# Cosine attention followed by a low-rank mixer: another order for the normalisation of the first heads, and six products spread over the MLP tiles

## The chip, the cores and the metric

One core of one Trainium2 chip. The metric is the time of one execution on the device in microseconds (us), the median of several runs. In three profiles (e2, e9 and c2) the matmul clock was granted at half for 3.4 us inside the ramp, from about 22 to 27 us; where it bears on a reading the text says so. A profiled execution's span is some 2 us below the timed figure of the same run (603.2 against 604.94 for the kernel before), so spans are compared with spans and times with times.

The profile's names: PE is TensorE (matmuls), ACT is ScalarE, DVE is VectorE, POOL is GpSimd, SP is SyncE. L577 is a line of the kernel; `attn<-sc` is the tile written and the tile read. A load *lands* when its data has arrived. The *ramp* is the time until PE is full, and the *rows* are the normalised rows of q and k.

## The reference, cut to what matters

```python
# q, k, v: 8 x 12 x 448 x 64 (batch, heads, tokens, width); C = 768
q_n = q / (norm(q) + 1e-6);  k_n = k / (norm(k) + 1e-6)
attn = softmax(q_n @ k_n.T / tau)          # tau = 0.1
x    = (attn @ v), heads side by side      # 8 x 448 x 768
u    = x + (x.T @ U @ V).T                 # low rank, 32, along the tokens
out  = u + relu(u @ w_ch1) @ w_ch2         # 768 -> 3072 -> 768
```

## The kernel before

The kernel doesn't fix the order of its instructions by hand. It hands operations with durations, dependencies and priorities to a small planner that simulates the engines and emits one order for each. A change of a dependency or priority re-plans the rest of the program, and once planned, each engine runs its own list in order.

Batch 0's twelve heads are normalised in four groups: the first pair (heads 0 and 1), the second pair, a third group of four heads and a fourth of four. Each group is squares, sums, ln and exp (for the root), an addition, a reciprocal, products with the rows:

```python
def squares(b, g, ld, ops, lo, ii, ss, pr, on, hold):
    for i in ii:                                   # q, k
        for a0 in range(0, g, G // 2):
            sq = Slot(r_sq, 1)                     # a ring of two buffers
            o = Op(on, ..., deps=[ops[i], *hold], acq=[sq], prio=pr + 0.2, fast=True)
            ...                                    # Square on ACT or x*x on DVE
            red.append(plan.add(Op("DVE", ..., reduce_sum(...),
                deps=[o], acq=[ss], rel=[sq], prio=pr + 0.1)))

def stats_first(ld, ops):                          # the first pair
    for i in range(2):
        done[i], up = scales(0, 0, 2, ld, ops, 0, (i,), inv, -1 - 0.1 * i, ("DVE", "ACT")[i])

# [...] order of the front:
second = load_qk(0, 2, 4, uses=2)
ld, ops, _ = load_qk(0, 4, 8)
begun = stats_first(*first[:2])
stats(0, 2, 4, *second, hold=begun)
xn_set.append(fill(memset of the third xn buffer, prio=0.2, deps=begun))
zf = fill(memset of the landing area of U and V, prio=0.1, acq=[uv], deps=begun)
stats(0, 4, 8, ld, ops, 0, hold=got[0, 0, "qkT"][2])
load_v0()
ld, ops, _ = load_qk(0, 8, 12)
late = stats(0, 8, 12, ld, ops, 0)
```

After batch 0's attention the MLP's long products start ("the block" below) and PE is full from there on. At MLP tile 9 the low-rank term is added for all tokens at once, three token tiles by two halves:

```python
def by_tokens(us, A, X):
    for i in range(3):
        for c0, c1 in ((0, CH), (CH, C)):
            mm = Slot(r_mm, 1)                     # a ring of three PSUM banks
            o = plan.add(Op("PE", ..., V_sb[...] x A[:, c0:c1] -> mm))
            plan.add(Op("DVE", ..., u = mm + X, deps=[o], rel=[mm, X], prio=2))
...
    if b == 0 and f == 9:
        by_tokens(us, *state["first"])
```

## Time and profile before

| | before |
|---|---|
| time, median of 3 runs | 605.15 us (604.89 to 605.44) |
| PE busy | 586.4 of 603.2 us |
| last exp of batch 0 ends (ACT) | 37.85 us |
| first long product of the MLP block (PE) | 41.3 us |

How to read it: in timelines each line has its start, its length (of a run of equal instructions), engine, source line, operation, tile, shapes, count, and in brackets the idle time before it with what ended it. The lines are in the prediction.

### The profile page before, as it was taken

What the parts mean: (1) busy time and instruction counts of PE and PEld (TensorE: products, weight loads), DVE (VectorE), ACT (ScalarE), POOL (GpSimd) and SP (SyncE); (2) the same over time, 40 slices, a digit from 0 to 9 for tenths busy, and PEclk for the clock granted to TensorE, in tenths of its full rate; (3) what the DMA queues carried; (4) which work ended last, traced back from release to release, by engine and by line L of the source; (5) the groups of instructions that cost most, each with busy time, mean ns of one, the idle gap of its engine ahead of it and who ended that gap; (6) DMA issues with size and microseconds to landing.
All of it is one profiled execution on the core that took longest, in us unless ns stands there. A gap on an engine that the chain in (4) does not pass through costs nothing.

```text
span 603.2 us, 11528 instructions
## 1 busy us (share of the span) xinstructions
PE 586.4 (97%) x4725; PEld 347.0 (58%) x4725; DVE 300.6 (50%) x728; ACT 276.9 (46%) x598; POOL 115.2 (19%) x175
## 2 busy tenths in 40 slices
PE   3899999999999999999999999999999999999997
PEld 1565666555565665666445666566545666654565
DVE  8979749989999988554731244014300210110011
ACT  5877652488874277316741067505642025014300
POOL 8246334062706116000600000000000000000000
PEclk9999999999999999999999999999999999999999
DMA  9999999999999959725922133030002110310021
GB/s 144 193 188 112 204 201 107 150 173 136 159 152 155 149 102 154 95 57 90 123 29 66 52 74 47 1 93 27 15 1 53 52 40 1 90 42 1 0 53 54
DMA packets 150165, 54.81 MB, mean 91 GB/s; under 512 B 115040, under 2 KB 150112, under 8 KB 150112
## 3 DMA queue, kind: packets, MB, share of 16 engines
q0 software_dynamic: 72864, 25.73, 38.4%
q1 hardware_dynamic: 77184, 28.32, 24.4%
q8 instruction: 37, 0.61, 0.4%
q14 instruction: 16, 0.13, 0.1%
q10 hardware_dynamic: 64, 0.02, 0.0%
HBM read 52.25 MB, written 11.01 MB: 105 GB/s over the span
## 4 chain that ended last, share of the span: by engine, by line
PE 93%; DVE 2%; ACT 2%; POOL 1%; DMA 1%; issue 0%; ACTq 0%; POOLq 0%
PE mm L794 36%; PE mm L760 35%; PE sc L572 10%; PE av L592 8%; PE mm L684 1%; PE tp L374 1%; DMA v_nat<-in_v_dram 1%; DVE xn L536 1%; PE mm L649 1%; POOL v_nat L429 1%; ACT attn L577 1%; PE sc L760 0%; POOL qk_nat L396 0%; DVE ss L461 0%; ACT qkT L824 0%
## 5 line engine op out<-in xcount | busy, mean ns | idle before, releaser
L760 PE MATMUL mm<-uT,w_sb 128*128 128x512 bf16 (+1 forms) x1134 | 241.3, 353 | 0.2 <-DVE u_nat L734 0.2
L794 PE MATMUL mm<-w_sb,relu 128*128 128x384 bf16 (+1 forms) x1368 | 231.3, 323 | 0.0
L577 ACT ACTIVATE attn<-sc 128x448 bf16<-128x448 f32 x336 | 164.6, 552 | 110.9 <-PE av L592 58.2
L794 PEld LDWEIGHTS <-relu 128*128 128x128 bf16 x1368 | 132.7, 98 | 86.1 <-issue 0.2
L760 PEld LDWEIGHTS <-w_sb 128*128 128x128 bf16 x1152 | 111.8, 98 | 102.7 <-issue 1.8
L783 ACT ACTIVATE relu<-mm 128x512 bf16<-128x512 f32 (+1 forms) x158 | 86.8, 549 | 129.3 <-PE mm L760 128.7
L803 DVE TENSOR_TENSOR O_sb<-mm,u_nat 128x384 f32<-128x384 f32 (+1 forms) x57 | 31.2, 549 | 210.8 <-PE mm L794 207.4
L572 PE MATMUL sc<-qkT 128*128 128x448 bf16 x336 | 102.7, 356 | 3.7 <-ACT attn L577 2.0
L592 PEld LDWEIGHTS <-attn 128*128 128x128 bf16 x1536 | 62.1, 98 | 17.8 <-issue 2.5
L418 POOL DMA_DIRECT2D v_nat<-in_v_dram x98 | 63.2, 655 | 31.7 <-DMA w_sb<-in_moe_w_ch_dram 15.8
L592 PE MATMUL av<-v_nat,attn 128*128 128x65 bf16 x1536 | 66.6, 194 | 0.8 <-DMA v_nat<-in_v_dram 0.4
L461 DVE TENSOR_REDUCE ss<-sq 112x8 f32<-112x512 bf16 x96 | 63.1, 673 | 0.2
L536 DVE TENSOR_TENSOR xn<-qk_nat,inv 112x512 bf16<-112x512 bf16 x94 | 60.9, 681 | 2.4 <-DMA qkT<-xn 2.2
L396 POOL DMA_DIRECT2D qk_nat<-in_q_dram x24 | 17.2, 718 | 136.5 <-DVE xn L536 117.0
L572 PEld LDWEIGHTS <-qkT 128*128 128x128 bf16 x336 | 28.9, 98 | 22.1 <-issue 7.3
L601 DVE TENSOR_TENSOR X_sb<-av,rd 128x256 bf16<-128x256 f32 x96 | 40.1, 419 | 1.6
L599 DVE RECIPROCAL rd<-av 128x4 f32<-128x4 f32 x96 | 17.1, 179 | 37.6 <-PE av L592 36.9
L457 DVE TENSOR_TENSOR sq<-qk_nat 112x512 bf16<-112x512 bf16 x87 | 33.7, 415 | 0.0
L698 DVE TENSOR_TENSOR u_nat<-mm,X_sb 128x384 bf16<-128x384 f32 x36 | 19.2, 553 | 15.4 <-PE mm L684 15.1
L785 DVE TENSOR_SCALAR relu<-mm 128x384 bf16<-128x384 f32 (+1 forms) x31 | 18.7, 604 | 12.8 <-PE mm L760 12.0
L374 PE MATMUL tp<-ident,xn 112*128 112x112 bf16 x144 | 11.9, 226 | 7.8 <-DVE xn L536 7.6
L474 ACT ACTIVATE ln<-ss 112x32 f32<-112x32 f32 (+2 forms) x26 | 6.0, 231 | 27.3 <-DVE ss L461 27.1
(61 smaller groups left out, 172.5 us busy)
## 6 DMA issues: line engine op xcount, KB each, us to landing
qk_nat<-in_q_dram POOLq DMA_DIRECT2D x23, 224.0 KB, 5.2
qk_nat<-in_k_dram POOLq DMA_DIRECT2D x23, 224.0 KB, 6.3
w_sb<-in_moe_w_ch_dram POOLq DMA_DIRECT2D x4, 1152.0 KB, 14.6
w_sb<-in_moe_w_ch_dram POOLq DMA_DIRECT2D x8, 576.0 KB, 15.8
out_dram<-O_sb SPq DMA_DIRECT2D x15, 168.0 KB, 2.2
out_dram<-O_sb SPq DMA_DIRECT2D x16, 144.0 KB, 2.1
out_dram<-O_sb SPq DMA_DIRECT2D x16, 120.0 KB, 2.0
out_dram<-O_sb SPq DMA_DIRECT2D x16, 96.0 KB, 2.2
```

Source lines behind the costliest of these rows:

```text
L418: nc.gpsimd.dma_start(out=vb[p0:p0 + s1 - s0, hs, j, 0:D], in_=v[b, hs].rearrange("h (s c) d -> c s h d", c=SC)[c, s0:s1]),
L457: nc.vector.tensor_mul(y, x, x)
L461: lambda i=i, a0=a0, a1=a1, sq=sq: nc.vector.reduce_sum(ss.tile[:, i, a0:a1, :].rearrange("p h c -> p (h c)"), sq.tile[:, 0:a1 - a0, :].re ...
L536: nc.vector.tensor_mul(dst, src, sc)
L572: nc.tensor.matmul(out=sc.tile[:, 0:S], lhsT=kT[:, 128 * m:128 * (m + 1)], rhs=qkT.tile[:, 8:12, :].rearrange("p c s -> p (c s)"), start=T ...
L577: exps[m] = plan.add(Op("ACT", act_t(S), lambda sc=sc, m=m: nc.scalar.activation(out=attn.tile[:, m, off:off + S], in_=sc.tile[:, 0:S], fu ...
L592: nc.tensor.matmul(out=av.tile[:, t, 0:D + 1], lhsT=attn.tile[:, m, 128 * t:128 * (t + 1)], rhs=v_t[b % 2][:, h, j, 0:D + 1], start=(j == ...
L601: muls.append(plan.add(Op("DVE", dve_t(256), lambda av=av, rd=rd, h=h: nc.vector.tensor_mul(X.tile[:, :, h * D:(h + 1) * D], av.tile[:, :, ...
L760: o = plan.add(Op("PE", pe_t(n), lambda cc=cc: nc.tensor.matmul(out=mm.tile[:, 0:n], lhsT=w1_sb[:, cc, f * 128:(f + 1) * 128], rhs=uT.tile ...
L783: nc.scalar.activation(out=relu.tile[:, f, 0:n], in_=mm.tile[:, 0:n], func=AF.Relu)
L794: nc.tensor.matmul(out=mm.tile[:, 0:c1 - c0], lhsT=relu.tile[:, f, i * 128:(i + 1) * 128], rhs=w2_t[:, f, c0:c1], start=(f == 0), stop=(f ...
L803: nc.vector.tensor_add(out=O.tile[:, 0:w], in0=mm.tile[:, 0:w], in1=us[i].tile[:, c0:c1]),
```

## The change

The intent: ACT squares both halves of the first pair; the second pair's sums and rows come next on DVE, ahead of two memsets and of the third group (`then`, `hold`), so that ACT gets its second pair of heads sooner; products with v are planned after v has landed; and the six products of `by_tokens` stand one at every second MLP tile.

```diff
-    done[i], up = scales(..., ("DVE", "ACT")[i])
+    done[i], up = scales(..., "ACT")
-    deps=[o], acq=[ss], rel=[sq], prio=pr + 0.1)))                # the sums
+    deps=[o, *then], acq=[ss], rel=[sq], prio=pr + 0.1)))
-    stats(0, 2, 4, *second, hold=begun)
-    xn_set.append(fill(..., prio=0.2, deps=begun))
-    zf = fill(..., prio=0.1, acq=[uv], deps=begun)
-    z  = fill(lambda: nc.vector.memset(V_sb, 0.0), 500, prio=-1.3)
+    begun_2 = stats(0, 2, 4, *second, hold=begun[:2], then=begun)
+    xn_set.append(fill(..., prio=0.41, deps=begun))
+    z  = fill(lambda: nc.vector.memset(V_sb, 0.0), 500, prio=3, deps=begun)
+    zf = fill(..., prio=0.5, acq=[uv], deps=begun)
-    stats(0, 4, 8, ld, ops, 0, hold=got[0, 0, "qkT"][2])
+    stats(0, 4, 8, *third, hold=last_exp["first"], then=begun_2)
-    LATE = 8.0                                # v: planned as landed after 2.0
+    LATE, VLATE = 8.0, 3.2                    # v: after 3.2; batch 0's q, k: 2.5 for 2.0
-    plan.add(Op("PE", 0.033, fn, ...          # a product with v, as planned
+    plan.add(Op("PE", 0.09 if b == 0 and p == 0 else 0.033, fn, ...
-    if b == 0 and f == 9:
-        by_tokens(us, *state["first"])
+    if b == 0 and 9 <= f < 21 and f % 2:
+        by_tokens(us, *state["first"], (f - 9) // 2)
[... the planner's rule for squares on ACT, the order of calls, signatures]
```

More of the change, by code (lines that the diff above doesn't have):

```diff
@@ L155, in run @@
                                 continue
-                            if e == "ACT" and o.fast and free["DVE"] <= t + 1e-9:
+                            if e == "ACT" and o.fast and "/" in o.eng and free["DVE"] <= t + 1e-9:
                                 continue
@@ L398, in load_qk @@
             in_=src[b, h0:h1].rearrange("h (s c) d -> s h (c d)", c=SC)),
-            (h1 - h0) * (0.31 if b else 0.35) + (1.2 if b == 0 and h0 == 4 and i == 0 else 0.0), acq=[ld], late=2.0 if b == 0 else LATE) for i, src in enumerate((q, k))]
+            (h1 - h0) * (0.31 if b else 0.35) + (1.2 if b == 0 and h0 == 4 and i == 0 else 0.0), acq=[ld], late=2.5 if b == 0 else LATE) for i, src in enumerate((q, k))]
         return ld, ops, lo
@@ L431, in part @@
                 in_=v[0, hs].rearrange("h (s c) d -> c s h d", c=SC)[c, s0:s0 + n]),
-                n * (0.0055 if hs.step == 2 else 0.011)))
+                n * (0.0055 if hs.step == 2 else 0.011), late=VLATE))
         for j in range(3):
@@ L440, in load_v0, with squares @@
             got[0, h, "v"] = ops
-    def squares(b, g, ld, ops, lo, ii, ss, pr, on, hold):
+    def squares(b, g, ld, ops, lo, ii, ss, pr, on, hold, then):
         red = []
@@ L464, in squares, with scales @@
                         axis=AX.X),
-                    deps=[o], acq=[ss], rel=[sq], prio=pr + 0.1)))
+                    deps=[o, *then], acq=[ss], rel=[sq], prio=pr + 0.1)))
         return red
-    def scales(b, h0, h1, ld, ops, lo, ii, inv, pr, on, hold=()):
+    def scales(b, h0, h1, ld, ops, lo, ii, inv, pr, on, hold=(), then=()):
         g = h1 - h0
         ss, ln, nv = Slot(r_ss, 1), Slot(r_ln, 1), Slot(r_ln, 1)
-        red = squares(b, g, ld, ops, lo, ii, ss, pr, on, hold)
+        red = squares(b, g, ld, ops, lo, ii, ss, pr, on, hold, then)
         w = slice(ii[0], ii[-1] + 1)
@@ L484, in scales, with stats @@
         return o, up
-    def stats(b, h0, h1, ld, ops, lo, hold=()):
+    def stats(b, h0, h1, ld, ops, lo, hold=(), then=()):
         pr = 0.3 + 0.03 * h0 if b == 0 else 4
         inv = Slot(r_inv, h1 - h0)
-        o, _ = scales(b, h0, h1, ld, ops, lo, (0, 1), inv, pr, "DVE" if b else "ACT/DVE", hold)
+        o, _ = scales(b, h0, h1, ld, ops, lo, (0, 1), inv, pr, "DVE" if b else "ACT/DVE", hold, then)
         for p in range(h0 // 2, h1 // 2):
@@ L499, in stats_first @@
         for i in range(2):
-            done[i], up = scales(0, 0, 2, ld, ops, 0, (i,), inv, -1 - 0.1 * i, ("DVE", "ACT")[i])
+            done[i], up = scales(0, 0, 2, ld, ops, 0, (i,), inv, -1 - 0.1 * i, "ACT")
             ups.append(up)
@@ L580, in attention @@
         last_exp[b] = exps[5]
+        if b == 0 and p == 0:
+            last_exp["first"] = [exps[1]]
         muls = []
@@ L595, in fn @@
                             rhs=v_t[b % 2][:, h, j, 0:D + 1], start=(j == 0), stop=(j == 3))
-                    o = plan.add(Op("PE", 0.033, fn,
+                    o = plan.add(Op("PE", 0.09 if b == 0 and p == 0 else 0.033, fn,
                         deps=need + got[b, h, "v"] + attn_set + [v_set[b % 2]] if first else (), acq=[av] if first else [],
@@ L723, in stage0, with by_tokens @@
         return us, uT, ut
-    def by_tokens(us, A, X):
-        for i in range(3):
-            for c0, c1 in ((0, CH), (CH, C)):
+    def by_tokens(us, A, X, part):
+        for i in range(part // 2, part // 2 + 1):
+            for c0, c1 in [((0, CH), (CH, C))[part % 2]]:
                 mm = Slot(r_mm, 1)
@@ L878, in att @@
     def att(b):
-        X = Slot(r_X, 0)
-        muls = []
-        for p in range(NPAIR):
+        X = Slot(r_X, 0) if b else X0
+        muls = [] if b else list(muls0)
+        for p in range(0 if b else 1, NPAIR):
             muls += attention(b, p, X)
@@ L889 @@
     second = load_qk(0, 2, 4, uses=2)
-    ld, ops, _ = load_qk(0, 4, 8)
+    third = load_qk(0, 4, 8)
     id_set = plan.add(Op("POOL", 0.8, lambda: make_identity(nc, ident)), pool_q)
-    begun = stats_first(*first[:2])
-    stats(0, 2, 4, *second, hold=begun)
-    xn_set.append(fill(lambda: nc.vector.memset(xn_t[2][:, 0:8, :], 0.0), 900, prio=0.2, deps=begun))
-    zf = fill(lambda: nc.vector.memset(U_f(), 0.0), 400, prio=0.1, acq=[uv], deps=begun)
+    load_v0()
+    fourth = load_qk(0, 8, 12)
+    v_set = [fill(lambda: set_v(v_t[0]), 1000, prio=-1.4)]
+    begun = stats_first(*first)
+    X0 = Slot(r_X, 0)
+    muls0 = attention(0, 0, X0)
+    begun_2 = stats(0, 2, 4, *second, hold=begun[:2], then=begun)
+    xn_set.append(fill(lambda: nc.vector.memset(xn_t[2][:, 0:8, :], 0.0), 900, prio=0.41, deps=begun))
+    z = fill(lambda: nc.vector.memset(V_sb, 0.0), 500, prio=3, deps=begun)
+    zf = fill(lambda: nc.vector.memset(U_f(), 0.0), 400, prio=0.5, acq=[uv], deps=begun)
     u0 = load_u(0)
@@ L899 @@
     u1 = load_u(1)
-    stats(0, 4, 8, ld, ops, 0, hold=got[0, 0, "qkT"][2])
-    load_v0()
-    ld, ops, _ = load_qk(0, 8, 12)
-    late = stats(0, 8, 12, ld, ops, 0)
+    stats(0, 4, 8, *third, hold=last_exp["first"], then=begun_2)
+    late = stats(0, 8, 12, *fourth)
     load_w1(0, 6)
     load_w1(6, 12)
-    v_set = [fill(lambda: set_v(v_t[0]), 1000, prio=-1.4),
-             fill(lambda: set_v(v_t[1]), 1000, prio=3, deps=late)]
+    v_set.append(fill(lambda: set_v(v_t[1]), 1000, prio=3, deps=late))
     consts = [plan.add(Op("POOL", 0.4, lambda: cast_u(0), deps=u0 + [z], rel=[uv]), pool_q),
```

## The prediction

> **What bounds the kernel now.** I read the page first, then the busy times by stretch, then the timelines of ACT, DVE and PE alone for the first 62 us, and last the chain of waits. The page says that PE is busy for 97% of the span, so only its gaps can be won:
>
> ```profile
> PE 586.4 (97%) x4725; PEld 347.0 (58%) x4725; DVE 300.6 (50%) x728; ACT 276.9 (46%) x598; POOL 115.2 (19%) x175
> ```
>
> The table by stretch says where they are. Columns: stretch, its length, then busy us of PE, PEld, DVE, ACT, POOL.
>
> ```profile
> 0.00:41.00 41.00, 28.74 (x346) 18.31 (x347) 34.97 (x105) 31.11 (x77) 21.98 (x36) 1.00 1.24 171
> 41.00:60.00 19.00, 17.98 (x138) 10.98 (x137) 17.45 (x37) 13.00 (x31) 11.76 (x18) 1.00 1.22 134
> 60.00:100.00 40.00, 39.99 (x417) 25.86 (x416) 28.15 (x74) 20.65 (x46) 15.40 (x23) 1.00 1.20 173
> ```
>
> PE idles 12.3 us before 41 us, 1.0 us from 41 to 60, nothing from 60 to 580, and 3.45 us in the last 23. So the change can act only on the first 60 us: the attention of batch 0, which must be over before its MLP can fill PE (at about 41.3 us), and the hand-over after it. Everything after 60 us slides by what is won there.
>
> In the ramp PE isn't the bound. From 5 to 30 us DVE is busy for 23.6 of 25 us and ACT for 20.2; from 30 to 38 ACT for 7.55 of 8. ACT's timeline has the bottleneck in it:
>
> ```profile
> 4.28 0.63 ACT L455 ACTIVATE sq<-raw_uv 112x512 bf16<-112x512 f32 x1 [2.26 <-DMA raw_uv<-in_k_dram]
> 8.83 0.66 ACT L824 COPY qkT<-tp 128x336 bf16<-128x336 bf16 x3 [1.03 <-PE tp L374]
> 10.62 0.63 ACT L455 ACTIVATE sq<-qk_nat 112x512 bf16<-112x512 bf16 x1 [1.14 <-DVE ss L461]
> 11.16 0.53 ACT L577 ACTIVATE attn<-sc 128x448 bf16<-128x448 f32 x1
> ...
> 14.01 1.01 ACT L577 ACTIVATE attn<-sc 128x448 bf16<-128x448 f32 x2
> 15.81 0.63 ACT L455 ACTIVATE sq<-qk_nat 112x512 bf16<-112x512 bf16 x1 [0.79 <-DVE ss L461]
> ...
> 18.14 1.40 ACT L577 ACTIVATE attn<-sc 128x448 bf16<-128x448 f32 x3
> ...
> 27.77 8.89 ACT L577 ACTIVATE attn<-sc 128x448 bf16<-128x448 f32 x19
> 36.87 0.98 ACT L577 ACTIVATE attn<-sc 128x448 bf16<-128x448 f32 x2 [0.20 <-PE sc L572]
> ```
>
> The reader should see three things. The first score starts on PE at 9.42 us, but its exp starts only at 11.16, because a square of the third group stands ahead of it in ACT's queue and waits for DVE to empty a buffer of squares. No exp starts between 15.02 and 18.14, since the second pair's scores aren't there. From 27.77 on, 21 exps run end to end, 0.468 us each (8.89/19): once the inputs exist ACT sets the pace, up to the last exp at 37.85.
>
> Why the second pair is late stands in DVE's timeline:
>
> ```profile
> 8.82 0.27 DVE L895 MEMSET raw_uv<- 128x256 f32 x1
> 9.15 0.48 DVE L894 MEMSET xn<- 112x512 uint32 x1
> 9.55 0.45 DVE L826 COPY qkT<-tp 128x336 bf16<-128x336 bf16 x3
> 9.91 1.27 DVE L461 TENSOR_REDUCE ss<-sq 112x8 f32<-112x512 bf16 x2
> 11.22 0.42 DVE L457 TENSOR_TENSOR sq<-qk_nat 112x512 bf16<-112x512 bf16 x1
> 11.56 1.27 DVE L461 TENSOR_REDUCE ss<-sq 112x8 f32<-112x512 bf16 x2
> 12.75 0.16 DVE L480 TENSOR_SCALAR ln<-ln 112x16 f32<-112x16 f32 x1
> ```
>
> Its sums (9.91) come after two memsets, and its scaling step (12.75) waits behind a square and two sums of the third group. Its normalised rows are written at 13.88 to 15.16 and its scores start at 17.65. The chain of waits names a third suspect: the products with v stand in PE's queue before v has landed (14.61), ahead of the second pair's transposes.
>
> **What the Trainium skill says.** "PSUM — Partial Sum Buffer", section "Engine vs sequencer instructions": the queues of ScalarE and VectorE are strictly first in, first out. The trace agrees: that is ACT's 1.14 us at 10.62. "ScalarE: Activation LUTs", section "What ACT_TABLE_LOAD costs": an activation with immediate operands takes 186 ns + 0.833 ns per element, and neighbours overlap by about 93 ns. For 512 elements that is 613 ns (the traced squares take 612 to 656), and for 448 it is 559 less 93 = 466 ns, against the 468 above. "VectorE: DVE Perf Modes", section "The perf-mode tier table": a product of two tensors runs at double rate in bf16 and single rate in fp32, a reduction always at single rate. Traced: squares of bf16 418 ns, of the fp32 first pair 620, sums of 512 elements 672. So the sums, not the squares, are DVE's heavy item. "DMA: Bandwidth & Descriptors", section "Issuing engines are not separate DMA queues": all issues share 16 engines, so later U and V loads compete with the MLP weights; the ramp already moves 171 GB/s.
>
> **The change part by part.**
>
> First, both squares of the first pair go to ACT, and the memset of V (0.30 us) leaves the front of DVE. q is issued at 0.74 and lands 2.9 us later, at 3.64; k at 1.18 + 3.1 = 4.28. ACT squares q from about 3.7 to 4.33 and k to 4.96, so ACT does in idle time what cost DVE 0.62. DVE, free at 4.11, sums q at 4.40 and k at 5.05, where it summed at 5.00 and 5.64 before. All of the first pair moves 0.6 us forward: last normalised rows at 7.9 instead of 8.51, first score at about 8.8. I use 0.6.
>
> Second, the second pair. The memset of the U and V landing area (0.27) drops behind its sums; the memset of a third buffer (0.48) stays ahead. Sums end at about 11.18 - 0.6 - 0.3 = 10.3. Ln and exp on ACT (0.21 each, with an exp of the softmax between) give 11.3; with no third-group work ahead, add and reciprocal give 11.8, and two products of 0.68 end at 13.1 instead of 15.16. Transposes, copies and scores follow as before, less the blocked products with v: scores at about 14 instead of 17.65.
>
> Third, ACT's total. From 10.62 to 37.85 is 27.2 us, of which 0.79 + 0.50 + 0.43 + 0.20 = 1.9 is idle, so 25.3 of work, unchanged in kind. The first exp can now start at about 9.2 instead of 11.16. With the old idle time repeated the last exp ends at 9.2 + 27.2 = 36.4; with half of it, at 35.5.
>
> Fourth, DVE's total, which must also fit. From 8.51 to the end of the fourth group's rows at 27.84 it was nearly gapless. It starts 0.6 earlier, takes in the V memset (0.3), and may lose some tenths while the third group is held. So the fourth group's rows end near 27.4, a gain of only about 0.4. But by then ACT should have two pairs of exps left (14 x 0.468 = 6.6) where it had 21 (9.8): 27.4 + about 1.2 for transpose, copy and score + 6.6 = 35.2.
>
> The ramp therefore ends at 35.2 to 36.4, say 35.8 for the last exp: 2.0 us won. The products with v, planned 1.2 us later (3.2 for 2.0), cost nothing and are part of this sum: PE's own wait for v was 0.44 us.
>
> Fifth, u by tokens. Six products and six DVE additions stood together at MLP tile 9. From 50.01 to 55.07 PE ran 12 products of 384 columns (0.163 each, from 1.79 us for 11 in the chain), 6 scores (0.19) and 8 transposes (0.05): 1.96 + 1.14 + 0.40 = 3.5 us of streaming in 5.06. About 1.5 is lost in that knot; the lines are:
>
> ```profile
> 50.01 1.17 PE L730 MATMUL mm<-A_sb,V_sb 128*128 128x384 bf16 x3
> ...
> 52.39 0.79 PE L730 MATMUL mm<-A_sb,V_sb 128*128 128x384 bf16 x2 [0.24 <-DVE u_nat L734]
> 53.91 0.81 PE L760 MATMUL mm<-uT,w_sb 128*128 128x384 bf16 x4 [0.19 <-DVE u_nat L734]
> ```
>
> The additions (0.55 us) wait behind sums (0.68) and hold the three PSUM buffers. One product at every second tile, some 2 us apart, leaves two free. Part of the 1.5 belongs to the scores that also sit there; I count 0.8.
>
> Sum: 2.0 + 0.8 = 2.8, and 605.15 - 2.8 = about 602.4 us.
>
> **The rivals.** (1) DVE is the bound of the ramp. Then only the first part counts: 0.3 to 0.6 us, plus the knot, giving 603.8 to 604.1. For it: DVE's 23.6 of 25 us. Against: DVE idles again after 30 us (4.95 of 8 busy) while ACT runs gapless to the end. (2) The loads move the wait. Casts of U and V wait for landings (16.05, 21.82 and 27.23), and POOL issues batch 1's q and k only after the last, at 27.94. The landing area is cleared after the second pair's sums, about 1.5 to 3 us later than 8.82, so batch 1's loads, weights and v slip alike. The first group of batch 1 was squared at 39.70, the weights had landed by 49.6, and V isn't needed before the first low-rank product near 36: slack of several us, but if the slip doubles, 1 to 2 us of the gain come back, giving 603.5 to 604.5. (3) ACT packs without gaps and the knot vanishes whole: 3.3 + 1.3, giving 600.6.
>
> **Range and chances.** My three ends of the ramp and two of the knot span 600.6 to 604.1; a re-planned order also shuffles the rest by some tenths. I take 600.6 to 604.3 with 602.4 as the centre. Two per cent is 12.1 us; PE's whole idle time is 16.8 us, 7.6 of it before the first transpose, so faster by 2% is practically excluded (0.01). Slower by 2% would need a new stall of 12 us (0.01). Within: 0.98.
>
> **What would show it.** First sums on DVE near 4.4; first exp on ACT near 9.2 with no square waiting ahead of it; second pair's scores near 14; last exp of batch 0 near 35.8; PE's low-rank products by tokens singly, with no wait on the additions. I'm wrong if the last exp stays past 37 (DVE or landings bind), if POOL's batch 1 loads land after DVE wants them, or if new gaps on PE appear after 60 us.

## The result, and the profile after

| | before | after |
|---|---|---|
| time, median | 605.3 us (604.89 to 605.69, 4 runs) | 604.35 us (603.66 to 604.86, 4 runs) |
| profiled span | 603.2 us | 602.4 us |

The ratio is 0.9984, with a 95% interval of 0.9966 to 1.0001. Ratios here are the mean time of one kernel's fast runs over that of the other's fast runs of the same rounds, so not quite the ratio of the medians. The interval includes 1, so these four runs alone don't show a gain clear of noise; the five-round repeat below (after_again, 0.9982, interval 0.9966 to 0.9998) just does. The forecast of 602.4 (600.6 to 604.3) missed: about 1 us came instead of 2.8.

The page's line of engines for the changed kernel. Not all matmul records are in the trace (4702 of 4725), so its PE sum is about 2 us too low:

```profile
PE 584.4 (97%) x4702; PEld 346.9 (58%) x4725; DVE 300.0 (50%) x722; ACT 278.8 (46%) x604; POOL 114.2 (19%) x175
```

Busy times by stretch of the changed kernel (the columns as in the prediction):

```profile
0.00:41.00 41.00, 29.48 (x348) 18.36 (x349) 34.66 (x100) 33.24 (x84) 20.93 (x35) 1.00 1.24 168
41.00:60.00 19.00, 18.70 (x146) 11.63 (x144) 17.50 (x37) 13.27 (x31) 11.53 (x17) 1.00 1.22 137
60.00:100.00 40.00, 39.23 (x427) 25.94 (x427) 29.43 (x75) 21.30 (x47) 15.65 (x24) 1.00 1.22 179
```

PE gained 0.74 us in the first stretch and 0.72 in the second, and lost 0.76 in the third, which had been gapless (some of it may be records that the trace lacks; the waits below are not). Three questions follow: why the ramp gave so little, what the spread gave, and what happened after 60 us.

**The ramp.** ACT's timeline in the changed kernel:

```profile
10.05 0.22 ACT L474 ACTIVATE ln<-ss 112x16 f32<-112x16 f32 x1 [0.47 <-DVE ss L461]
10.17 0.53 ACT L577 ACTIVATE attn<-sc 128x448 bf16<-128x448 f32 x1
...
18.65 0.54 ACT L577 ACTIVATE attn<-sc 128x448 bf16<-128x448 f32 x1 [0.16 <-PE sc L572]
19.09 0.62 ACT L455 ACTIVATE sq<-qk_nat 112x512 bf16<-112x512 bf16 x1
20.42 1.03 ACT L826 COPY qkT<-tp 128x672 bf16<-128x672 bf16 x3 [0.70 <-PE tp L374]
21.62 1.03 ACT L826 COPY qkT<-tp 128x672 bf16<-128x672 bf16 x3 [0.17 <-PE tp L374]
22.52 0.58 ACT L577 ACTIVATE attn<-sc 128x448 bf16<-128x448 f32 x1
...
26.99 4.51 ACT L577 ACTIVATE attn<-sc 128x448 bf16<-128x448 f32 x10
31.81 4.25 ACT L577 ACTIVATE attn<-sc 128x448 bf16<-128x448 f32 x9 [0.31 <-PE sc L572]
36.27 0.98 ACT L577 ACTIVATE attn<-sc 128x448 bf16<-128x448 f32 x2 [0.20 <-PE sc L572]
```

The hole without exps from 15.0 to 18.1 has shrunk to one from 13.9 to 15.3, and another has opened from 19.2 to 22.5: ACT finishes the second pair's exps 2.6 us earlier (19.19 for 21.80) and then has none until the third group arrives. From 26.99 on there are 10 + 9 + 2 = 21 exps left, as many as before at 27.77. The last exp ends at 37.25, for 37.85 before and 35.8 forecast.

Why the third group didn't come sooner begins in DVE's timeline of the changed kernel:

```profile
14.62 1.46 DVE L461 TENSOR_REDUCE ss<-sq 112x8 f32<-112x512 bf16 x2
16.59 0.76 DVE L457 TENSOR_TENSOR sq<-qk_nat 112x512 bf16<-112x512 bf16 x2 [0.51 <-DMA qk_nat<-in_q_dram]
17.27 0.68 DVE L461 TENSOR_REDUCE ss<-sq 112x8 f32<-112x512 bf16 x1
17.86 0.17 DVE L480 TENSOR_SCALAR ln<-ln 112x32 f32<-112x32 f32 x1
17.95 0.68 DVE L461 TENSOR_REDUCE ss<-sq 112x8 f32<-112x512 bf16 x1
18.54 0.34 DVE L482 RECIPROCAL inv<-ln 112x32 f32<-112x32 f32 x1
18.80 0.36 DVE L457 TENSOR_TENSOR sq<-qk_nat 112x512 bf16<-112x512 bf16 x1
19.08 2.48 DVE L536 TENSOR_TENSOR xn<-qk_nat,inv 112x512 bf16<-112x512 bf16 x4
```

The third group's sums end at 16.1, but its rows start at 19.08, against 18.99 before. Squares and sums of the fourth group stand ahead of its addition (17.86) and reciprocal (18.54), and the first of these squares waits 0.51 us for the fourth group's q to land. That isn't the whole of it: the addition also needs ACT's ln and exp of the third group, and the exp, itself between exps of the softmax, ends only at 17.59. So the addition could have come 0.3 us sooner at most; the experiments come back to this.

**The spread.** In PE's timeline of the changed kernel the products by tokens stand singly and wait for nothing:

```profile
49.41 0.32 PE L732 MATMUL mm<-A_sb,V_sb 128*128 128x384 bf16 x1
...
53.99 0.33 PE L732 MATMUL mm<-A_sb,V_sb 128*128 128x384 bf16 x1
...
58.02 0.33 PE L732 MATMUL mm<-A_sb,V_sb 128*128 128x384 bf16 x1
```

**After 60 us.** PE's waits from 60 to 112 us, changed kernel (what waited, for what, then total, times, longest). The same answer for the kernel before has no entry:

```profile
PE tp L374 <- ACT uT L826: 0.7, 1, 0.7
PE mm L796 <- DVE O_sb L805: 0.3, 1, 0.3
PE tp L374 <- ACT qkT L826: 0.3, 1, 0.3
PE sc L686 <- issue: 0.2, 1, 0.2
```

Two of these places, first in the kernel before, then in the changed one:

```profile
96.41 1.95 PE L794 MATMUL mm<-w_sb,relu 128*128 128x384 bf16 x11
98.19 0.67 PE L592 MATMUL av<-v_nat,attn 128*128 128x65 bf16 x16
98.71 1.30 PE L794 MATMUL mm<-w_sb,relu 128*128 128x384 bf16 x7
...
104.28 0.39 PE L374 MATMUL tp<-ident,u_nat 128*128 128x128 bf16 x4
104.50 1.30 PE L794 MATMUL mm<-w_sb,relu 128*128 128x384 bf16 x7
105.64 0.42 PE L374 MATMUL tp<-ident,u_nat 128*128 128x128 bf16 x4
```

```profile
95.95 1.46 PE L796 MATMUL mm<-w_sb,relu 128*128 128x384 bf16 x8
97.74 0.32 PE L796 MATMUL mm<-w_sb,relu 128*128 128x384 bf16 x1 [0.32 <-DVE O_sb L805]
...
103.25 0.39 PE L374 MATMUL tp<-ident,u_nat 128*128 128x128 bf16 x4
104.31 0.38 PE L374 MATMUL tp<-ident,u_nat 128*128 128x128 bf16 x4 [0.67 <-ACT uT L826]
```

Before, sixteen products with v fill the time that DVE needs to empty the three PSUM banks of the first group of down products, and seven down products lie between the two fours of transposes. In the changed order both fillers are gone from there, and PE waits.

**A yardstick for what follows.** Where two kernels have the same work for PE in another order, I compare the times at which each has begun exactly the same set of matmuls. The difference to the kernel before's trace I call the distance (negative is ahead). For the changed kernel it is -0.60 at the block (constant from 41 to 49 us), -1.90 at 76.8 us of the kernel before, -1.45 at 81.4, and -0.75 at the last matmul. So in this pair of profiles the ramp won 0.60, the spread 1.30, and 1.15 was given back. What follows the ramp, the end less the block, is -0.15. The changed kernel's missing records leave no such points between 91 us and the end. In its repeat, after_again, whose trace is complete, the distance is +0.01 at the block, -1.23 at 76.8, then +0.44 at 106 us, 1.67 lost in three steps at the places of the three waits (0.44, 0.49 and about 0.8), and -0.09 at the end: 0.53 is won back between 130 and 232 us, for which I have found no cause.

### The profile page after: what moved, and what is told of

Read it like the earlier page. It is cut to its first block, busy times and chain, and to the rows that moved or that the text cites. A ratio compares the mean times of both kernels' runs of the same rounds, so it can differ in the third digit from the quotient of the medians.

```text
span 602.4 us, 11513 instructions
## 1 busy us (share of the span) xinstructions
PE 584.4 (97%) x4702; PEld 346.9 (58%) x4725; DVE 300.0 (50%) x722; ACT 278.8 (46%) x604; POOL 114.2 (19%) x175
## 4 chain that ended last, share of the span: by engine, by line
PE 91%; DVE 4%; DMA 2%; ACT 1%; issue 1%; POOL 1%; ACTq 0%; DVEq 0%; POOLq 0%
PE mm L796 36%; PE mm L762 34%; PE sc L572 10%; PE av L594 8%; PE mm L686 1%; DVE xn L536 1%; DMA v_nat<-in_v_dram 1%; DMA qk_nat<-in_q_dram 1%; DVE ss L461 1%; PE tp L374 1%; PE mm L651 1%; ACT attn L577 1%; PE sc L762 0%; POOL qk_nat L396 0%; ACT relu L785 0%
## 5 line engine op out<-in xcount | busy, mean ns | idle before, releaser
L762 PE MATMUL mm<-uT,w_sb 128*128 128x384 bf16 (+1 forms) x1112 | 236.7, 353 | 1.2 <-ACT relu L785 0.2
L572 PE MATMUL sc<-qkT 128*128 128x448 bf16 x336 | 104.4, 361 | 3.1 <-ACT attn L577 1.5
## 6 DMA issues: line engine op xcount, KB each, us to landing
w_sb<-in_moe_w_ch_dram POOLq DMA_DIRECT2D x8, 576.0 KB, 16.2
```

The lines of the kernel that those rows point to most:

```text
L572: nc.tensor.matmul(out=sc.tile[:, 0:S], lhsT=kT[:, 128 * m:128 * (m + 1)], rhs=qkT.tile[:, 8:12, :].rearrange("p c s -> p (c s)"), start=T ...
L762: o = plan.add(Op("PE", pe_t(n), lambda cc=cc: nc.tensor.matmul(out=mm.tile[:, 0:n], lhsT=w1_sb[:, cc, f * 128:(f + 1) * 128], rhs=uT.tile ...
```

## The experiments

All sixteen runs in one table, under the two kernels. "Fourth" is where DVE's (with * ACT's) first square of the fourth group starts, "third rows" where DVE's first normalised rows of the third group start, "block" where the fifth of the long products starts; the distance at the block is this less 41.29. "End" is the distance at the last matmul, "rest" the end less the distance at the block.

| run | fourth | third rows | block | end | rest | time (ratio) |
|---|---|---|---|---|---|---|
| before | 15.81* | 18.99 | 41.29 | 0 | 0 | 605.3 |
| after | 16.59 | 19.08 | 40.69 | -0.75 | -0.15 | 604.35 (0.9984) |
| after_again | 17.18 | 19.67 | 41.31 | -0.09 | -0.11 | 604.6 (0.9982) |
| e1_spread_only | 16.83* | 19.90 | 42.27 | +0.11 | -0.87 | 604.65 (0.9985) |
| e2_no_spread (half clock 22.1 to 25.5) | 16.83 | 19.42 | 41.28 | +0.54 | +0.55 | 605.33 (0.9994) |
| e3_sums_halved | 16.43 | 18.70 | 40.49 | -0.96 | -0.15 | 603.97, once |
| e4_sums_twice | 17.11 | 19.71 | 41.32 | -0.13 | -0.16 | 604.9, once |
| e5_exps_twice_early | 16.33 | 19.61 | 41.22 | -0.23 | -0.15 | 604.71, once |
| e6_exps_twice_late | 15.86 | 18.69 | 41.13 | -0.27 | -0.11 | 604.75, once |
| e7_pool_memsets | 15.52 | 18.09 | 39.71 | -2.04 | -0.46 | 604.12 (0.9978) |
| e8_fillers | 15.92 | 18.77 | 40.41 | -0.75 | +0.14 | 604.24 (0.9977) |
| v1_even | 16.24 | 18.73 | 40.34 | -1.51 | -0.57 | 603.55 (0.9968) |
| e9_fourth_first (half clock 23.6 to 27.0) | other order | 20.75 | 43.68 | +1.41 | -0.97 | 605.97 (1.0007) |
| c1_pool_fourth | other order | 19.84 | 41.88 | -0.39 | -0.97 | 605.22 (0.9995) |
| e10_hold_fourth | 21.18 | 18.48 | 40.78 | -1.62 | -1.11 | 603.65 (0.9969) |
| e11_hold_pool | 20.51 | 17.79 | 40.88 | -1.02 | -0.61 | 604.61 (0.9983) |
| c2_pool_even (half clock 21.8 to 25.2) | 16.75 | 19.34 | 41.08 | +0.78 | +0.99 | 605.15 (0.9987) |
| c3_hold_pool_even | 20.35 | 17.64 | 40.52 | -0.46 | +0.31 | 604.59 (0.9985) |

In e2, e10 and e11 the execution goes on 0.2 to 0.3 us longer after the last matmul than in the others, so their spans profit less than "end" says.

Three things stand out before any single run. Six runs whose program after the ramp is the changed kernel's own (after, after_again, e3 to e6) have a rest of -0.11 to -0.16: it belongs to the order of instructions and repeats to within 0.1 us. Three more with the spread, but another front (e1, e9, c1), have -0.87 to -0.97. The distance at the block, by contrast, moves by 0.6 us between two profiles of one kernel. And where the front is the changed kernel's, the block follows the third group's rows: it comes 21.6 us after they start in after, after_again, e4, e5, e7, e8 and v1 (21.9 in e2 with its half clock, 21.8 in e3, 22.4 in e6 with its extra exps after the rows), while in the old front (before, e1) it takes 22.3 to 22.4. So with this order what delays these rows delays the end of the ramp.

### What sets the ramp's end (e3 to e6)

The theories were ACT's total work, DVE's total work, and the landing of the loads. e3 halves what the sums of the third and fourth groups read. Its output is wrong, which doesn't matter for the time. e4 repeats the two sums of the third group's q. e5 repeats two exps of the second pair, e6 two exps of the fifth.

```diff
 # e3: batch 0, groups of four heads
-    sq.tile[...].rearrange("p h (c d) -> p (h c) d", d=D)
+    sq.tile[...].rearrange("p h (c d) -> p (h c) d", d=D)[:, :, 0:32]
 # e4: reduce_sum(...)  ->  [reduce_sum(...) for _ in range(2)]   third group, q
 # e5: activation(Exp)  ->  twice, pair 1, first two
 # e6: activation(Exp)  ->  twice, pair 4, first two
```

> Wrong result on purpose: the eight sums of the third and fourth group of batch 0 add only half of each row; the order of all instructions stays that of the changed kernel. About 8 x 0.27 = 2.1 us less work for DVE before 24 us. Theory D (DVE sets the ramp until the fourth group's rows are written, ACT after that): the last four products of the fourth group start 1 to 2 us before 24.74 us, and the first long block of MLP products starts 1 to 2 us before 40.69 us. Rival A (ACT's total sets the ramp, as I predicted): that block moves by less than 0.3 us.

> Two sums of the third group are done twice (+1.3 us of DVE work near 13 to 15 us), order otherwise that of the changed kernel. Theory D: the first long block of MLP products comes 1.0 to 1.3 us later than 40.69 us. Rival A: less than 0.4 us later.

> Two exps of the second pair are done twice (+0.94 us of ACT work near 15 us), order otherwise that of the changed kernel. Theory D: ACT has slack there, so the first long block of MLP products moves by less than 0.3 us from 40.69 us. Rival A: it moves by about 0.9 us.

> Two exps of the fifth pair are done twice (+0.94 us of ACT work after 28 us), order otherwise that of the changed kernel. Theory D and rival A both say that ACT sets the pace there: the first long block of MLP products moves by about 0.9 us from 40.69 us. A third theory, that DVE sets the pace to the end of the ramp, says less than 0.3 us.

Measured: e3's block stood at 40.49, 0.20 before the changed kernel's, although DVE had some 2 us less to do; the fourth group's q had landed 0.16 earlier there, so hardly anything is left for the shorter sums. Its first sums of the third group were shorter, and the time went into a longer wait at the same place in DVE's queue:

```profile
16.43 0.76 DVE L457 TENSOR_TENSOR sq<-qk_nat 112x512 bf16<-112x512 bf16 x2 [0.74 <-DMA qk_nat<-in_q_dram]
```

So DVE's work alone isn't the bound. But e4's 1.34 us more of DVE moved the block by 0.63 against the changed kernel, while its wait of 0.51 at that place was gone; e5's 0.94 us more of ACT moved it by 0.53; e6's 0.94 us moved it by 0.44, but there, too, next to no time went on waiting for the fourth group's q. The run e8 below has the same ramp as the changed kernel and no such wait (block at 40.41). Measured from it, e4's work cost 0.91 and e6's 0.72. So more work on either engine costs some 0.7 to 0.8 of itself (0.91 of 1.34, 0.72 of 0.94), and less work on one of them wins nothing while the other or a landing holds. No single bound explains all four runs. e4 and e5 cost what they do by making the third group's rows late (19.71 and 19.61, against 18.77 in e8), e6 by what ACT has to do after them. These are one profile each, at landings that differ.

### The landing (after_again, e9, c1)

The changed kernel once more, timed in five rounds; and the fourth group's load issued ahead of v's, alone (e9) and with e7's edit below (c1).

```diff
 # e9, c1
-    load_v0()
     fourth = load_qk(0, 8, 12)
+    load_v0()
```

> The changed kernel once more, beside the others on the same chip: 603.5 to 605 us. The landing of the fourth group has come between 15.8 and 16.9 us in the traces so far; I expect the first long MLP block to shift with it by some tenths around 40.69 us, and everything after 42 us to keep its distances to within 0.1 us, the three waits after 75 us included.

> The changed kernel with the loads of the fourth group of batch 0 issued before those of v. Theory L (in the ramp DVE waits for the landing of the fourth group, whose squares stand in its queue ahead of the third group's scaling): that wait (0.5 us at 16.59) goes, third group's rows start 0.5 to 1.0 us before 19.08, first long MLP block 0.3 to 0.9 us before 40.69. If v's later landing (near 17 us) takes its place, PE's products with v wait and the block is not earlier. The total depends on the order again: its eight transposes in a lump cost some 0.7 us.

> Both ramp edits together: two memsets by POOL and the fourth group loaded before v. If DVE's work and the landing each hold the ramp in part, first long MLP block at 39.2 to 39.7 us, against 39.73 with the memsets alone. The order has the lump of eight transposes (0.7 us), so the total is near 602.5 to 603.5 us.

Measured: after_again repeated the time (604.6) and the rest (-0.11), but its block stood at 41.31, since its fourth group waited longer:

```profile
17.18 0.76 DVE L457 TENSOR_TENSOR sq<-qk_nat 112x512 bf16<-112x512 bf16 x2 [1.24 <-DMA qk_nat<-in_q_dram]
```

Over the runs with the changed ramp the block follows this start: 15.92 gives 40.4 and 16.24 40.3, 16.59 gives 40.7, 16.83 gives 41.3 (e2, with PE at half clock for 3.4 us in its ramp), 17.18 gives 41.3. Below 16.2 nothing more comes of it, and the traces show why: the third group's addition stands 1.27 us behind this square (16.59 and 17.86), and when the square comes early enough the addition waits for ACT's exp of the group instead. e8's line:

```profile
17.54 0.18 DVE L481 TENSOR_SCALAR ln<-ln 112x32 f32<-112x32 f32 x1 [0.28 <-ACT ln L478]
```

In the profile of the changed kernel, then, the landing cost about 0.3 us, and the rest of the ramp's miss (1.1 of 1.4 us) isn't its doing. Part of the late landing is a late issue: POOL, behind v's loads in its queue, issued this load at 11.60 in after and at 12.76 in after_again, and it landed at 16.50 and 17.09.

The kernel before depends on it as well. e1 has its front; the fourth group's q landed at 15.73 in before and at 16.75 in e1, and the block came at 41.29 and 42.27. So the two profiled kernels weren't alike in this: at like landings the changed front is ahead by some 0.9 us (41.29 against e8's 40.41 and v1's 40.34) to 1.0 (e1 against e2, whose half clock works against it), and not by 0.60. That fits the timed gain of about 1 us better than the 0.75 of the profiles. With two profiles of the old front it is an indication.

Issuing the fourth group first was a miss: the block came at 43.68. The planner, which now expected the fourth group's q early, put its first square at the head of DVE's queue, and DVE stood still for it ahead of the second pair's scaling. The instruction waits for the semaphore of the fourth group's load, which landed at 11.46; the third group's q had landed at 9.09:

```profile
11.56 0.42 DVE L457 TENSOR_TENSOR sq<-qk_nat 112x512 bf16<-112x512 bf16 x1 [1.16 <-DMA qk_nat<-in_q_dram]
```

The third group's rows started at 20.75. The half clock from 23.6 us on adds to this block by an amount that I can't give. c1, at full clock, lost in the ramp as well (0.68 us at the same square). An early issue with the old order of squares wasn't tried.

### Taking that wait out of DVE's queue (e10), and DVE's memsets away (e7, e11)

e7 puts two memsets (0.48 and 0.30 us) on GpSimd. e10 releases the fourth group's squares only after the third group's rows. e11 does both.

```diff
 # e7
-    fill(memset of the third xn buffer and of V, on DVE)
+    Op("POOL", nc.gpsimd.memset(...))       # after the loads in its queue
 # e10
-    stats(0, 4, 8, *third, hold=last_exp["first"], then=begun_2)
-    late = stats(0, 8, 12, *fourth)
+    third_rows = stats(0, 4, 8, *third, hold=last_exp["first"], then=begun_2)
+    late = stats(0, 8, 12, *fourth, hold=third_rows)
```

> The changed kernel with the two memsets of the third buffer of normalised rows (0.48 us) and of V (0.30 us) done by POOL in its idle time near 15 us in place of DVE. Theory D: the ramp ends a further 0.4 to 0.8 us earlier (first long MLP block at 39.9 to 40.3 us); its order has filler at both later waits, so total 2.3 to 2.9 us below the kernel before. Rival A: ramp as in the changed kernel.

> Changed kernel, the fourth group's squares (on ACT and DVE) released only by the third group's last normalised rows. Theory landing-in-the-queue (the fourth group's landing, met in DVE's queue, is what holds the third group's scaling): the third group's first rows, 19.1 in the changed kernel, come at 18.0 to 18.6 whatever the landing, DVE shows no wait for in_q at 16 to 17 us, and the first long MLP block comes at 39.9 to 40.4 instead of 40.7. Rival, total work (DVE's and ACT's sums only change places): third rows earlier by the same amount, but the fourth group's rows end at 28 or later instead of 27.3, and ACT, which runs dry between, ends no sooner: block at 40.7 to 41.5. After the ramp the order is a new one, so the rest may shift by up to 0.7 either way; time 603.5 to 605.

> e10 with the memsets of the third buffer and of V on GpSimd (0.8 us less for DVE). Theory landing-in-the-queue: block at 39.3 to 39.9, at least 0.5 before e10's. Rival, total work: it gains the same over e10 as e7 did over the changed kernel after allowing for the landing (0.3 to 0.6), and no more than e7's own 39.8.

Measured: e7's block came at 39.71, with no wait for a landing (15.52): 0.7 before e8's, whose landing was no hindrance either. So work taken from DVE does count where the landing doesn't hold it. It is one profile, and of e7's fastest run (602.91; its six runs lie between that and 606.09); in c2, with the same memsets moved, the fourth group's square came at 16.75 and the block at 41.08 (with the half clock).

e10 is the run that tells most about the ramp. DVE's timeline, then ACT's, of e10:

```profile
14.55 1.34 DVE L461 TENSOR_REDUCE ss<-sq 112x8 f32<-112x512 bf16 x2
17.43 0.30 DVE L480 TENSOR_SCALAR ln<-ln 112x32 f32<-112x32 f32 x1 [1.54 <-ACT ln L477]
...
18.48 2.48 DVE L536 TENSOR_TENSOR xn<-qk_nat,inv 112x512 bf16<-112x512 bf16 x4
...
27.18 1.99 DVE L536 TENSOR_TENSOR xn<-qk_nat,inv 112x512 bf16<-112x512 bf16 x3
```

```profile
28.97 2.03 ACT L826 COPY qkT<-tp 128x672 bf16<-128x672 bf16 x6
30.75 6.58 ACT L577 ACTIVATE attn<-sc 128x448 bf16<-128x448 f32 x14
```

The wait for the landing is gone and the third group's rows start 0.6 us earlier, at 18.48. But DVE now stands 1.54 us for ACT's ln and exp instead, the fourth group's rows start at 27.18 instead of 24.74 (the last of their four products, beyond the window shown, ends at 29.77), and the block comes at 40.78, no sooner than before the edit. The rival, that the work only changes places, was right, and the place in the queue was not what bounds the ramp. The 14 exps left at 30.75 are exactly the "two pairs left" that the prediction had counted on at 27.4 + 1.2; they are reached 2.2 us later, since the fourth group's rows now end at 29.77 and not at 27.4. e11's expected further gain of 0.5 in the ramp didn't come either (rows at 17.79, block at 40.88).

e10's time is nevertheless 603.65, a good half microsecond or more below the changed kernel. By the table that isn't the ramp: its rest is -1.11, for -0.15 (by spans -0.91). The edit re-planned everything after it, and this order has only two short waits on PE between 60 and 112 us:

```profile
PE mm L762 <- ACT qkT L826: 0.3, 1, 0.3
PE sc L686 <- DVE u_nat L697: 0.2, 1, 0.2
```

### The two halves of the change (e1, e2, v1)

e1 is the kernel before with the spread alone, e2 the changed kernel without it, v1 the changed kernel with the products at even tiles.

```diff
 # e1: before.            # e2: after, reversed.
-    if b == 0 and f == 9:
-        by_tokens(us, *state["first"])
+    if b == 0 and 9 <= f < 21 and f % 2:
+        by_tokens(us, *state["first"], (f - 9) // 2)
 # v1
-    if b == 0 and 9 <= f < 21 and f % 2:
+    if b == 0 and 10 <= f < 22 and f % 2 == 0:
```

> The kernel before with only u by tokens spread over the MLP tiles. Theory: the spread itself wins about 1.5 us by 70 us (the knot from 50 to 54 us is gone), and the ramp stays (first long MLP block at 41.29 us). After that PE's order has no filler at two places where it waits for a PSUM bank: after the first group of MLP down products (no product with v stands there), and in eight transposes of u_nat in one lump. Each costs about 0.6 us, so the total is only 0.2 to 0.5 us below the kernel before. Rival (the spread costs nothing later): 1.3 to 1.6 us below.

> The changed kernel without the spread. Theory: first long MLP block at 40.69 us (0.6 us won), the knot is back, and the same two places without filler cost about 1.2 us, so the total is 0.3 to 0.8 us above the kernel before. Rival (what the ramp wins is kept): 0.6 us below it.

> The changed kernel with the six products of u by tokens at tiles 10, 12, ... 20 in place of 9, 11, ... 19; the work is the same. In its order sixteen products with v stand right after the first group of down products, and the last eight transposes of u_nat are split into four and four; one lump of sixteen is left. Theory (the give-back is the accident of which work stands at the two waits): 2.1 us won by 70 us, at most 0.6 given back, total 1.5 to 2.1 us below the kernel before. Rival (the give-back is structural: PE's gain is used up by waits for DVE in batch 1 whatever the order): about 0.7 to 0.9 us below, as the changed kernel.

Measured: the times are 604.65, 605.33 and 603.55. e1's rest is -0.87: of some 1.3 won at the knot (the six products that stood together at MLP tile 9) two thirds stay. e2's rest is +0.55, so the new order of the front alone costs half a microsecond further on (one wait of transposes on DVE's writing of O is 0.7 us long; e1, c1 and e9 have it too). The two rests add up to -0.32, where the whole change has -0.11 to -0.15. e2's time can't be told from the kernel before's (0.9994, interval 0.9983 to 1.0006). v1, an equally arbitrary choice of tiles, has a rest of -0.57 and the best time of all. Against the kernel before, by the ratios, e1 is 0.9 us faster (0.2 to 0.5 expected), e2 0.4 faster within its noise (0.3 to 0.8 slower expected) and v1 1.9 faster, as its theory had it (1.5 to 2.1): the give-back depends on the order and isn't a fixed cost.

### Repairing the three waits by hand (e8)

PE's order alone, after planning: eight down products ahead of the sixteen products with v, seven between the fours of transposes, five MLP products ahead of the twelve transposes that start at 76.2.

```diff
     order = plan.run()
+    for move in [(880, 8, 864), (946, 7, 942), (715, 5, 697)]:
+        forward(*move)        # n of PE's operations, from here, to there
```

> The changed kernel with nothing but three moves in PE's order, at the three new waits of the changed kernel's trace (75.58, 97.11 and 103.65 us): 5, 8 and 7 products of the MLP that are ready anyway are put ahead of, or between, what waits there. Theory (the give-back is which work stands at a wait for a PSUM bank, an accident of the order): the three waits of together some 1.8 us go, and the kernel is 1.0 to 1.8 us faster than the changed kernel in the same rounds. Rival (structural: DVE and ACT are behind in batch 1 whatever PE does): the waits come back elsewhere, less than 0.4 us faster.

Measured: 604.24, in time no different from the changed kernel in the same rounds (0.9977 and 0.9982), and a rest of +0.14, worse by 0.3 than without the repair. The three waits are gone, but PE's waits from 60 to 112 us in e8 are now:

```profile
PE mm L797 <- DVE O_sb L806: 1.2, 1, 1.2
```

And the cause of the larger one, in e8's DVE timeline:

```profile
97.43 0.18 DVE L602 RECIPROCAL rd<-av 128x4 f32<-128x4 f32 x1 [1.10 <-PE av L595]
97.53 0.15 DVE L481 TENSOR_SCALAR ln<-ln 112x32 f32<-112x32 f32 x1
97.65 0.42 DVE L604 TENSOR_TENSOR X_sb<-av,rd 128x256 bf16<-128x256 f32 x1
97.99 1.47 DVE L806 TENSOR_TENSOR O_sb<-mm,u_nat 128x384 f32<-128x384 f32 x3
```

The products with v came later, so DVE's reciprocal of their sums waited 1.10 us for them, and behind it in the same queue stood the addition that empties the PSUM banks. PE then waited 1.20 us for that. An order of one engine is only good together with the orders of the others.

### Do the gains add up? (c2, c3)

c2 is e7 with v1's tiles, c3 the same with e10's hold.

```diff
 # c2 = e7 + v1;  c3 = e7 + e10 + v1 (edits as above)
```

> The two memsets on GpSimd and the products by tokens at the even tiles 10 to 20: if ramp and what follows add up, 604.35 less 0.5 (e7's share beyond its landing) less 0.4 to 0.8 (even tiles): 603.0 to 603.5. If the order after the ramp is shuffled by every edit, as the runs so far say, 603.5 to 604.6.

> All three edits. Adding up: 602.5 to 603.2; shuffled: 603.2 to 604.6.

Measured: 605.15 and 604.59. They don't add up: c2's rest is +0.99, the worst of all, c3's +0.31. Each edit re-plans what follows, and the re-plan is worth anything between -1.1 and +1.0. The best versions found are v1 (603.55, ratio 0.9968, interval 0.9955 to 0.9981) and e10 (603.65, 0.9969, interval 0.9957 to 0.9982), which can't be told apart; both beat the kernel before by about 1.9 us and have medians some 0.7 to 1.0 us below the changed kernel's, though their intervals overlap with its own. c2's 0.99 is made of waits after the ramp (0.8, 0.7 and 0.5 us are the longest), not of its half clock, which fell before the block.

## Why the prediction was wrong

**First part, the first pair: right in kind.** DVE's first sum came at 4.27 (forecast 4.40), the first score at 8.95 (8.8), so 0.47 of the 0.6 us.

**Second part, the second pair: nearly right.** Its scores came at 14.72 (forecast about 14, before 17.65).

**Third part, ACT's total: missed by 1.45 us.** The forecast was 9.2 for the first exp plus 26.3 to 27.2 for the rest, 35.8 in the middle; the last exp ended at 37.25. The first exp came at 10.17, 1.0 late: ahead of it in ACT's queue stood copies of keys and the second pair's ln, which waited 0.47 us for DVE's sums. The stretch from there to the last exp's end was 27.08. The sum had a slip too: its 27.2 ran from the square at 10.62; from the first exp, at 11.16, it was 26.7 in the kernel before, so the stretch grew. Of its idle time, 1.54 us were left (0.16 + 0.70 + 0.17 + 0.31 + 0.20), so the step "with half of it" didn't come true. The cost of an exp was not at fault: nine of 448 elements took 4.25 us in the changed kernel, 0.472 each, beside the estimate of 466 ns from the Trainium skill's page "ScalarE: Activation LUTs", section "What ACT_TABLE_LOAD costs".

**Fourth part, the step that failed.** "So the fourth group's rows end near 27.4" was right: they ended at 27.24. "But by then ACT should have two pairs of exps left (14 x 0.468 = 6.6) where it had 21" was wrong. There were 21 again. The second pair's exps were earlier by 2.6 us, but ACT could not go on to the third pair, whose rows came no earlier (19.08 for 18.99). What the step left out is when the third group's rows arrive: ACT stood without exps until then, and in seven profiles of the changed front the block follows 21.6 us after them. Moving one group forward in a chain of two full engines shrank the hole from 15.0 to 18.1 and opened one from 19.2 to 22.5. Rival 1, DVE as the bound of the ramp with a gain of 0.3 to 0.6, gave the size of this pair of profiles (0.60), which is partly luck, since at like landings the gain is 0.9 or more. I had argued it away with DVE's idle time after 30 us, when the matter is decided before 19 us. e4 to e6 show that its wording is too narrow: ACT and DVE both hold, and the landing adds 0.3 here and up to 0.9 in other runs.

**Fifth part, the knot: right mechanism, size off.** 0.8 was counted, 1.3 came (-0.60 to -1.90), most of the 1.5 lost there. My reserve for scores that also sit there was too large.

**"Everything after 60 us slides by what is won there": wrong.** At 76.8 us the kernel was 1.90 ahead, of the 2.8 of the sum, and 1.15 net was given back, with 1.67 lost at three waits in the complete trace. No rival had this, though the prediction named new gaps on PE after 60 us as a sign that it would be wrong. The kernel before had no wait at all there; the prediction counted "some tenths" for a new order, and the runs show up to about 1 us either way.

In sum, for the profiled pair: ramp 0.60 for 2.0, knot 1.30 for 0.8, give-back 1.15 for 0, total 0.75, and about 1 in the timed runs.

**Rival 2, the loads of batch 1: harmless.** They were issued at 28.28 for 27.94 before. (The first product that reads V came at 37.37 in the kernel before, not near 36.) The chances (0.98 within 2%) held.

**What stays open.** The parts of the new front (ACT's squares, the hold, the memsets' places, the later plan for v) weren't run one by one, so the ramp's gain isn't split among them. How much of the ramp belongs to ACT and how much to DVE isn't a question with one answer while they wait for each other; e10 shows the wait changing hands. Why v's and the fourth group's loads come later in one profile than in the next wasn't tried; nor was a spread of orders planned on purpose, so which property of an order makes its rest good isn't known.

## What to carry to other kernels

When two engines feed each other through queues, moving one group forward moves the gap to the group behind it: count what the engine has left when the last group arrives, and look up when the group in between arrives, not only the one that was moved. In a kernel whose bottleneck engine is gapless after some point, treat that as something a new order need not have: any re-planning upstream can lose it, so check the far end of the trace for new waits before believing an early gain. And where repeated profiles of one kernel differ by as much as the edit, split the trace into the part that repeats (0.1 us here) and the part that doesn't (0.6 us), and compare kernels on the first.

## What the Trainium skill lacked or had wrong

- "PSUM — Partial Sum Buffer", section "Engine vs sequencer instructions", says that the queues of ScalarE and VectorE are strictly first in, first out, and the runs agree. What it lacks is the consequence for reordering: three moves in PE's queue alone turned a wait of 0.32 us into one of 1.20, through an unrelated reciprocal ahead in DVE's queue.
- "DMA: Bandwidth & Descriptors": I found no word in it, or on another page, on how much the landing of one kernel's load varies between executions. In two profiles of the same kernel the fourth group's first square, which waited for it, started at 16.59 and 17.18, and the end of the ramp moved with it by 0.6 us.
- No page has a figure for what a changed order of a planned program costs downstream. Here it was between -1.1 and +1.0 us of 604, and repeated to 0.1 us for the same order.
